# First loads of a two-branch attention kernel: 64-row slices by one broadcast DMA each, on other queues

## The chip, the cores and the metric

The kernel runs on one core of a Trainium2 chip. The time is the device time of one execution in microseconds (us), the median of several runs; a profile of one execution comes with it. Engines are called PE (matmuls; PEld is its weight load), DVE, ACT, POOL and SP. DMAs are issued by SP and ACT (hardware queues) and by POOL (software queue).

## The reference

Two attention branches over the same X (2048 rows, 576 columns, 32 heads of 18) are mixed by a gate per row. Branch A has its own keys and values for each head, branch B shares one key and one value head.

```python
g = sigmoid((x * gate_w).sum(-1, keepdims=True))
qkv = (x @ wqkv).reshape(B, S, 3, H, Dh)          # branch A
a = softmax(q @ k.T * Dh**-0.5) @ v               # per head, then @ wo
b = softmax((x @ wq) @ (x @ wk).T * Dh**-0.5) @ (x @ wv)   # then @ B_wo
return g * a + (1 - g) * b
```

All inputs are float32, and the kernel gets near float32 precision from matmuls in a rounded format (fp32r): each operand is written as a rounded high part h and a low part l = value - h, and a product takes h·h, l·h and h·l.

## The kernel before

X comes transposed (576 rows of 2048), and all projection weights but A's values come as one array `wall` of 14 row tiles, each 576 x 128. The contraction length 576 is cut into four groups of 128 (512 rows) and a fifth of 64 rows, the **slice** (rows 512 to 575). In the fifth group the 64 rows stand twice, in partitions 0 to 63 and again in 64 to 127, so that one matmul over 128 partitions does two of the three products for them: `xh[64:128, 4]` is overwritten with X's low part (L222).

`load5` (L120) fetches such a tile: the 512 rows as one DMA that SP issues (the main part), then the 64-row slice by two DMAs, one for each half of the partitions, on the queue that the argument `rest` names (SP if it is left out). `load_w` (L129) fetches a weight tile into `wst`, `load_x` (L211) a piece of X: the first two pieces are half chunks of 256 columns (`xsh`), the next three chunks of 512 (`xs`, two buffers, so the third waits until the first of them is rounded). The order is written out by hand at L224 to L237: weight tile 0 and the two half chunks with their slices on POOL's queue; six matmuls on constants that keep PE busy (L230); weight tiles 1 and 2, slices on POOL's queue as well; then the three chunks and weight tiles 3 to 5, all on SP.

`prep_w` (L134) rounds a weight tile on ACT (L126) and takes the low part on DVE (L127). `split_x` (L216) rounds 256 columns of X on ACT (L220) and takes low parts on DVE (L221, L222). The loop at L245 runs over the four chunks of 512 columns: row tiles 0, 1 and 2 are projected for each chunk (`project`, L142: matmuls of L150 into `ps`; for the first chunk row tile 0 goes in two halves of 256 columns), and within it the next chunk is rounded. A projection leaves through ACT (L154) and DVE (L160) and is written to `qk` in DRAM by a DMA of POOL (L161); for some also a `kd` write (L167). Row tiles 3 to 13 follow (`project_rest`, L268), each over all four chunks, with weight tiles fetched three row tiles ahead. After that come the attention steps, which the change doesn't touch.

The tile framework gives every DMA of the hardware queues one of eight completion semaphores in turn; the ninth waits until the first has landed, and so on. DMAs of POOL have eight of their own.

Of the kernel before, what the change touches and what calls it, by code (L numbers as in the profile page):

```python
# [11 lines left out]
AF = mybir.ActivationFunctionType  # L12
# [30 lines left out]
def gated_mix_kernel(ctx: ExitStack, tc: tile.TileContext, xT, wall, wv, wo, out):  # L43
    nc = tc.nc
    P = 128

    def dma(o, i, eng=None):
        o, i = (x.bitcast(F32) if x.dtype == F32R else x for x in (o, i))
        return (eng or nc.sync).dma_start(o, i)
# [27 lines left out]
    ones = fixed.tile([P, 32], F32, name="ones")  # L77
# [3 lines left out]
    nc.vector.memset(acc, 0.0)  # L81
    nc.vector.memset(vb, 1.0)
    nc.vector.memset(ones, 1.0)
    nc.scalar.activation(ones, ones, AF.Copy)

# [31 lines left out]

    def load5(t, src, rest=None):  # L120
        dma(t[:, 0:4, :], src[0:512, :].rearrange("(p k) m -> p k m", p=P))
        dma(t[0:64, 4, :], src[512:576, :], rest)
        dma(t[64:128, 4, :], src[512:576, :], rest)

    def split_w(st, w, eng_l):
        nc.scalar.activation(w["h"], st, AF.Copy)  # L126
# [2 lines left out]
    def load_w(mt, rest=None):  # L129
        st = wpool.tile([P, NKT, P], F32, name="wst", bufs=6)  # L130
        load5(st, wall[mt], rest)
        return st

    def prep_w(st):  # L134
        w = {y: wpool.tile([P, NKT, P], F32R, name=f"w{y}", bufs=3) for y in "hl"}
        split_w(st, w, nc.vector)
        return w
# [4 lines left out]
    def project(mt, c, w, parts=1):  # L142


        fp = ps_s.tile([P, 512], F32, name="ps")
        cs = slice(c * 512, (c + 1) * 512)
        g = 512 // parts
        for i in range(parts):
            for n, (a, b, k, kr) in enumerate(PROJ):
                nc.tensor.matmul(fp[:, g * i:g * i + g], w[a][:kr, k, :],  # L150
                                 X[b][:kr, k, c * 512 + g * i:c * 512 + g * i + g],
                                 start=(n == 0), stop=(n == len(PROJ) - 1))
        hl = stp.tile([P, 2, 512], F32R, name="phl", bufs=4)
        nc.scalar.activation(hl[:, 0, :], fp, AF.Copy)  # L154
        if mt == 0 or c == 0 and mt in HAS_K:
            st = stp.tile([P, 512], F32, name="pst", bufs=3)
            nc.scalar.activation(st, fp, AF.Copy)
            if c == 0:
                KD[mt] = st
        nc.vector.tensor_tensor(hl[:, 1, :], fp, hl[:, 0, :].bitcast(F32), op=OP.subtract)  # L160
        dma(qk_d[:, mt * P:(mt + 1) * P, cs].rearrange("a p f -> p a f"), hl, nc.gpsimd)  # L161
        if c == 1 and mt in HAS_K:
            d = stp.tile([P, 512], F32, name="pd", bufs=1)
            nc.vector.tensor_tensor(d, fp, KD.pop(mt), op=OP.subtract)
            dhl = stp.tile([P, 2, 512], F32R, name="pdhl", bufs=1)
            split(d, dhl[:, 0, :], dhl[:, 1, :], nc.scalar, nc.vector)
            dma(kd_d[:, mt * P:(mt + 1) * P, :].rearrange("a p f -> p a f"), dhl, nc.gpsimd)  # L167
        if mt == 0:
            dma(z_d[cs], st[ROW_G:ROW_G + 1, :])
            return c, st  # L170

    def shared_v(c, st):
        pv = ps_m.tile([P, 512], F32, name="pm")
        for j in range(4):
            nc.tensor.transpose(pv[:, 18 * j:18 * j + 18],  # L175
                                st[ROW_VB:ROW_VB + 18, j * P:(j + 1) * P],
                                ident[ROW_VB:ROW_VB + 18, ROW_VB:ROW_VB + 18])
        nc.vector.tensor_copy(vb[:, 4 * c:4 * c + 4, 0:18],
                              pv[:, 0:72].rearrange("p (j d) -> p j d", d=18))
# [28 lines left out]
    with tc.tile_pool(name="xs", bufs=1, side="right") as xsp:  # L208
        XS = []

        def load_x(c, rest=None):  # L211
            half = c < 2
            XS.append(xsp.tile([P, NKT, 256 if half else 512], F32, name="xsh" if half else "xs", bufs=2))
            load5(XS[c], xT[:, 256 * c:256 * c + 256] if half else xT[:, 512 * (c - 1):512 * c], rest)

        def split_x(c):  # L216
            xs = XS[c // 2 + 1][:, :, 256 * (c % 2):256 * (c % 2) + 256] if c > 1 else XS[c]
            cs = slice(c * 256, (c + 1) * 256)
            xh = X["h"][:, :, cs]
            nc.scalar.activation(xh, xs, AF.Copy)  # L220
            nc.vector.tensor_tensor(X["l"][:, :, cs], xs[:, 0:4], xh[:, 0:4].bitcast(F32), op=OP.subtract)  # L221
            nc.vector.tensor_tensor(xh[64:128, 4], xs[64:128, 4], xh[64:128, 4].bitcast(F32), op=OP.subtract)  # L222

        W = [load_w(0, nc.gpsimd)]  # L224
        load_x(0, nc.gpsimd)
        load_x(1, nc.gpsimd)

        warm = ps_m.tile([P, 512], F32, name="pm")
        for i in range(6):
            nc.tensor.matmul(warm[:, 0:304], ident, vb.rearrange("p k d -> p (k d)"), start=True, stop=True)  # L230
        W.append(load_w(1, nc.gpsimd))
        W.append(load_w(2, nc.gpsimd))
        for c in range(2, 5):
            load_x(c)
        dma(ones_r.rearrange("a (b c) -> (a b) c", c=32), ones)
        for mt in range(3, 6):
            W.append(load_w(mt))  # L237
        for t in vst:
            nc.gpsimd.memset(t, 1.0)
        WP = [prep_w(W.pop(0))]  # L240
        split_x(0)
        split_x(1)
        WP.append(prep_w(W.pop(0)))
        WP.append(prep_w(W.pop(0)))
        for c in range(4):  # L245
            keep = project(0, c, WP[0], 2 if c == 0 else 1)
            if c == 3:
                WN = prep_w(W.pop(0))
            project(1, c, WP[1])
            if c < 3:  # L250
                split_x(2 * c + 2)
                split_x(2 * c + 3)
            shared_v(*keep)
            project(2, c, WP[2])
    vwp = ph1.enter_context(tc.tile_pool(name="vwp", bufs=1, side="right"))

    def load_wv(hf):
        VS[hf] = vwp.tile([P, NKT, 288], F32, name="vwst")
        load5(VS[hf], wv[:, 288 * hf:288 * hf + 288])
# [409 lines left out]
    for T in range(0, NSTEP + 2, 2):  # L669
# [7 lines left out]
        for op in (FIRST if T == 0 else ALONE if alone else UNIT if units else PLAIN).split():  # L677
            k, second, c = op[0], op[1:2] == "B", op[2:]
# [61 lines left out]
```

## Time and profile before

| | us |
|---|---|
| median of 3 runs | 2768.68 (2768.68 to 2769.95) |
| the profiled execution | 2769.62 |
| its span, first to last instruction | 2767.8 |
| PE busy | 2755.4 |
| DVE busy | 2420.0 |
| ACT busy | 2432.1 |
| POOL busy | 214.9 |

The mean granted clock of PE was 0.998 of full speed. Times in the views count from the span's start. A row of the timeline has start, length, engine, line, operation, tiles and shapes, and in brackets the idle time before it and what ended it. A row of a window view has the stretch, its length, busy time and instructions of PE, PEld, DVE, ACT and POOL, then the granted clock, the mean busy share of the 16 DMA engines and their GB/s. A row of DMA issues has the tiles, the queue, how many, the size of one and, for POOL, the time to landing. POOL's two DMAs for one slice count as two.

### The profile page before, as it was taken

How to read it: one execution, taken by the hardware profiler on the slowest of the kernel's cores; microseconds unless marked ns; L12 is line 12 of the kernel's file. 1: busy time of each engine (PE TensorE's matmuls, PEld its weight loads, DVE VectorE, ACT ScalarE, POOL GpSimd, SP SyncE). 2: the span in 40 equal slices, each digit the busy share in tenths (PEclk: the TensorE clock that was granted, in tenths of full speed). 3: DMA queues.
4: the chain of work that ended last, by engine and by line, in shares of the span. 5: the costliest groups of instructions: out<-in, count | busy, mean ns of one | idle time of the engine just before them, and what ended most of it. 6: DMA issues, size and time to landing. Idle time of an engine off the chain costs nothing.

```text
span 2767.8 us, 57564 instructions
## 1 busy us (share of the span) xinstructions
PE 2755.4 (100%) x22158; PEld 1226.9 (44%) x22158; DVE 2420.0 (87%) x4495; ACT 2432.1 (88%) x4776; POOL 214.9 (8%) x349
## 2 busy tenths in 40 slices
PE   9999999999999999999999999999999999999999
PEld 7888333333333333333333444444444443334554
DVE  4347999999999999999999999999999999998873
ACT  3332999999999999999999999999999999998776
POOL 2220000011001000100110001000100010011000
PEclk9999999999999999999999999999999999999999
DMA  7762011121112111211143234232332223234412
GB/s 250 251 227 74 24 32 27 32 59 53 34 30 63 42 32 35 72 39 32 40 108 99 70 76 105 61 83 71 88 85 77 70 80 84 66 77 120 110 35 87
DMA packets 122962, 214.51 MB, mean 78 GB/s; under 512 B 53500, under 2 KB 80716, under 8 KB 111002
## 3 DMA queue, kind: packets, MB, share of 16 engines
q1 hardware_dynamic: 108256, 170.79, 23.6%
q0 software_dynamic: 9824, 35.07, 3.4%
q10 hardware_dynamic: 4608, 4.98, 0.5%
q8 instruction: 174, 2.85, 0.4%
q14 instruction: 100, 0.82, 0.1%
HBM read 137.23 MB, written 64.77 MB: 73 GB/s over the span
## 4 chain that ended last, share of the span: by engine, by line
PE 99%; DVE 0%; DMA 0%; ACT 0%; POOL 0%; issue 0%; DVEq 0%; POOLq 0%; ACTq 0%
PE ps L402 42%; PE acc L416 39%; PE ps L150 7%; PE pm L367 5%; PE pm L542 4%; PE ps L186 2%; DMA xsh<-xT 0%; PE ps L367 0%; PE pm L402 0%; DVE mx L376 0%; DVE oacc L554 0%; PE pm L569 0%; PE ps L592 0%; ACT pt L409 0%; PE pm L175 0%
## 5 line engine op out<-in xcount | busy, mean ns | idle before, releaser
L409 ACT ACTIVATE pt<-ps 128x512 f32<-128x512 f32 x4052 | 2129.8, 613 | 104.0 <-PE pm L367 46.4
L376 DVE TENSOR_REDUCE mx<-pm 128x1 f32<-128x512 f32 x3064 | 1957.0, 684 | 138.8 <-PE pm L367 95.2
L402 PE MATMUL ps<-qs,ksb 56*128 56x512 f32 x2688 | 906.9, 436 | 0.3
L367 PE MATMUL pm<-ksb,qs 54*128 54x512 f32 x2332 | 813.4, 443 | 0.0
L402 PEld LDWEIGHTS ps<-qs,ksb 56*128 56x128 f32 x2688 | 436.5, 184 | 688.4 <-ACT pt L409 669.3
L416 PE MATMUL acc<-pt,vb 128*19 128x256 f32 (+1 forms) x6144 | 592.4, 457 | 0.1
L416 PE MATMUL acc<-pt,vg 128*19 128x256 f32 (+1 forms) x5656 | 579.4, 481 | 0.4 <-DVE oe L428 0.4
L402 PE MATMUL ps<-qs,ksa 56*128 56x512 f32 x1364 | 456.3, 437 | 0.0
L367 PE MATMUL pm<-ksa,qs 54*128 54x512 f32 x1232 | 433.4, 443 | 0.0
L367 PEld LDWEIGHTS pm<-ksb,qs 54*128 54x128 f32 x2332 | 375.2, 184 | 2.2
L402 PEld LDWEIGHTS ps<-qs,ksa 56*128 56x128 f32 x1364 | 218.4, 184 | 344.2 <-ACT pt L409 316.8
L373 DVE CUSTOM_DVE_ANT_0 junk<-pm,xb 128x512 bf16<-128x512 f32 x500 | 340.3, 681 | 0.2 <-ACT xb L370 0.2
L370 ACT ACTIVATE xb<-pm 128x512 f32<-128x512 f32 x500 | 305.1, 610 | 0.0
L367 PEld LDWEIGHTS pm<-ksa,qs 54*128 54x128 f32 x1232 | 200.4, 184 | 0.7
L416 PEld LDWEIGHTS acc<-pt,vb 128*19 128x19 f32 x6144 | 104.2, 97 | 209.2 <-issue 199.1
L416 PEld LDWEIGHTS acc<-pt,vg 128*19 128x19 f32 x5656 | 96.5, 97 | 208.2 <-issue 195.4
L367 PE MATMUL pm<-kdb,qs 54*128 54x512 f32 x372 | 148.5, 399 | 0.0
L116 POOL CAST mh<-mt 128x32 fp32r<-128x32 f32 x64 | 13.4, 210 | 1696.0 <-DVE mt L384 1696.0
L154 ACT ACTIVATE phl<-ps 128x512 fp32r<-128x512 f32 x56 | 33.5, 597 | 104.4 <-PE ps L150 75.6
L160 DVE TENSOR_TENSOR phl<-ps,phl 128x512 fp32r<-128x512 f32 x56 | 38.7, 692 | 94.7 <-ACT phl L154 70.9
L150 PE MATMUL ps<-xh,wh 128*128 128x512 f32 (+1 forms) x285 | 83.7, 392 | 4.9 <-ACT xh L220 4.9
L150 PE MATMUL ps<-xh,wl 128*128 128x512 f32 (+1 forms) x285 | 82.9, 389 | 0.0
(107 smaller groups left out, 1373.6 us busy)
## 6 DMA issues: line engine op xcount, KB each, us to landing
qs<-qk SPq DMA_DIRECT2D x384, 144.0 KB
qk<-phl POOLq DMA_DIRECT2D x56, 512.0 KB, 4.1
ksa<-qk SPq DMA_DIRECT2D x132, 144.0 KB
ksb<-qk SPq DMA_DIRECT2D x66, 144.0 KB
onh<-oh SPq DMA_DIRECT2D x32, 256.0 KB
onl<-ol SPq DMA_DIRECT2D x32, 256.0 KB
oih<-onh SPq DMA_DIRECT2D x16, 512.0 KB
oil<-onl SPq DMA_DIRECT2D x16, 512.0 KB
```

Of the source, the lines that this page charges most:

```text
L150: nc.tensor.matmul(fp[:, g * i:g * i + g], w[a][:kr, k, :], X[b][:kr, k, c * 512 + g * i:c * 512 + g * i + g], start=(n == 0), stop=(n == ...
L154: nc.scalar.activation(hl[:, 0, :], fp, AF.Copy)
L160: nc.vector.tensor_tensor(hl[:, 1, :], fp, hl[:, 0, :].bitcast(F32), op=OP.subtract)
L186: nc.tensor.matmul(fp[:, 0:288], X[b][:kr, k, st_ * P:(st_ + 1) * P], w[a][:kr, k, :], start=(n == 0), stop=(n == len(PROJ) - 1))
L367: nc.tensor.matmul(pm, qs[u % 3][b:b + 54, i * P:(i + 1) * P], k, start=True, stop=True)
L370: nc.scalar.activation(MX["x", u, i], pm, AF.Relu)
L373: nc.vector.tensor_tensor_reduce(junk, pm, MX.pop(("x", u, i)), 1.0, -3e38, op0=OP.add, op1=OP.max, accum_out=MX[u][:, i, c:c + 1])
L376: nc.vector.tensor_reduce(MX[u][:, i, c:c + 1], pm, axis=AX.X, op=OP.max)
L402: nc.tensor.matmul(ps, kst(u)[b:b + 56, i * P:(i + 1) * P], qs[u % 3][b:b + 56, c * 512:(c + 1) * 512], start=True, stop=True)
L409: nc.scalar.activation(pt, ps, AF.Exp, scale=SCALE)
L416: nc.tensor.matmul(acc[32 * j:32 * j + 19, a:b], v_of(u, i), PT[u, i, j][:, a:b], start=(i == 0), stop=(i == 15), skip_group_check=True)
L542: nc.tensor.matmul(fp[:, 0:288], o[b][:r, t, s2 * P:(s2 + 1) * P], w[a][:r, t, 288 * hf:288 * hf + 288], start=(n == 0), stop=(n == 3 * nt ...
```

## The change

The slice comes by one DMA, whose source is a broadcast of the 64 rows to two copies. The slices of weight tile 0 and of the two half chunks of X are issued by ACT, those of weight tiles 1 and 2 by SP, like the later ones. ACT's first activation (a copy of `ones` onto itself, which brings ACT's table load with it) moves from the very start to behind ACT's three DMAs. Of the first 256 columns of X, ACT rounds groups 0 to 2 and DVE groups 3 and 4. Since ACT's and SP's DMAs share the eight semaphores of the hardware queues, in the built program the main part and the slice of weight tile 2 wait for the slice and the main part of weight tile 0; the main parts and slices of the first two full chunks wait likewise for those of the two half chunks.

```diff
-    nc.scalar.activation(ones, ones, AF.Copy)
...
     def load5(t, src, rest=None):
         dma(t[:, 0:4, :], src[0:512, :].rearrange("(p k) m -> p k m", p=P))
-        dma(t[0:64, 4, :], src[512:576, :], rest)
-        dma(t[64:128, 4, :], src[512:576, :], rest)
+        dma(t[:, 4, :], src[512:576, :].unsqueeze(0).to_broadcast([2, 64, src.shape[1]]), rest)
...
-            nc.scalar.activation(xh, xs, AF.Copy)
+            if c == 0:
+                nc.scalar.activation(xh[:, 0:3], xs[:, 0:3], AF.Copy)
+                nc.vector.tensor_copy(xh[:, 3:5], xs[:, 3:5])
+            else:
+                nc.scalar.activation(xh, xs, AF.Copy)
...
-        W = [load_w(0, nc.gpsimd)]
-        load_x(0, nc.gpsimd)
-        load_x(1, nc.gpsimd)
+        W = [load_w(0, nc.scalar)]
+        load_x(0, nc.scalar)
+        load_x(1, nc.scalar)
+        nc.scalar.activation(ones, ones, AF.Copy)
...
-        W.append(load_w(1, nc.gpsimd))
-        W.append(load_w(2, nc.gpsimd))
+        W.append(load_w(1))
+        W.append(load_w(2))
```

## The prediction

> **What bounds the kernel now.** I read the page first, for the engine that carries the chain.
>
> ```profile
> span 2767.8 us, 57564 instructions
> PE   9999999999999999999999999999999999999999
> PE 99%; DVE 0%; DMA 0%; ACT 0%; POOL 0%; issue 0%; DVEq 0%; POOLq 0%; ACTq 0%
> ```
>
> TensorE (PE) is busy in every slice and 99% of the chain is its own work. Whatever delays PE once delays the end by as much; whatever lies beside it costs nothing. The change touches only the opening, so I read the chain of waits there (start, length, what), and the matmuls that open each chunk of 512 columns in the timeline.
>
> ```profile
> 2.74 0.50 POOL xsh L49
> 3.25 8.08 DMA xsh<-xT
> ...
> 11.40 1.28 ACT xh L220
> ...
> 12.72 8.86 PE ps L150 x42
> ```
>
> ```profile
> 1.92 5.90 PE L230 MATMUL pm<-vb,ident 128*128 128x304 f32 x12 [1.92 <-DVE ones L83]
> 6.83 0.74 ACT L126 ACTIVATE wh<-wst 128x640 fp32r<-128x640 f32 x1 [4.57 <-DMA wst<-wall]
> 22.11 2.43 ACT L220 ACTIVATE xh<-xs 128x1280 fp32r<-128x1280 f32 x2
> 25.18 1.07 PE L150 MATMUL ps<-xh,wh 128*128 128x512 f32 x4
> 35.30 1.07 PE L150 MATMUL ps<-xh,wh 128*128 128x512 f32 x4
> 45.41 1.07 PE L150 MATMUL ps<-xh,wh 128*128 128x512 f32 x4
> ```
>
> The only load that PE waits for is the first half chunk of X: its 64-row slice, issued by POOL, lands at 11.3 us, ACT rounds it, and PE, idle since 7.82 (1.92 + 5.90), starts at 12.72. From there PE goes on without a stop: chunk 1 starts at 25.18, chunk 2 at 35.30, chunk 3 at 45.41, 10.12 apart. Chunk 1 is rounded by ACT from 22.11 to 24.54, 0.6 us before PE takes it; chunks 2 and 3 go the same way.
>
> **The change, part by part.** *How many DMA engines a slice uses.* Before, a slice is two DMAs of 64 rows. After, it is one whose source is a broadcast: in the built program it reads as 2 copies, 64 rows, columns, with the 2 outermost and of stride zero. Before has no such load of 2 copies, but it has a broadcast of one row to 18 (R, L49), with 18 outermost. These stretches hold only that and other 18-row loads (DMA share, GB/s at the end of a row):
>
> ```profile
> 598.00:600.00 2.00, 2.00 (x16) 0.62 (x14) 1.83 (x5) 1.78 (x5) 0.00 (x0) 1.00 0.58 139
> 600.00:602.00 2.00, 2.00 (x24) 0.77 (x24) 2.00 (x4) 2.00 (x5) 0.00 (x0) 1.00 0.61 156
> ...
> 604.00:606.00 2.00, 2.00 (x22) 0.76 (x24) 2.00 (x4) 1.95 (x5) 0.00 (x0) 1.00 0.61 143
> ...
> R<-r_d SPq DMA_DIRECT2D x7, 144.0 KB
> ```
>
> With these loads queued the share stays at 0.58 to 0.61, where the stretches below, with 16 engines at work, show 1.02 to 1.09. That is 9 of 16 engines (0.56 times 1.02 to 1.09 is 0.57 to 0.61), and 9 is the largest divisor of 18 below 16. So the outermost count limits the engines, and a zero stride doesn't lift that. I take **2 engines** for every slice of the changed kernel. The other end, 16, is possible, because no row shows a load whose source says 2 and whose destination says 128; it is rival A.
>
> *What one engine moves.* Loads of the opening, the weights among others, with all 16 at work:
>
> ```profile
> 2.00:3.00 1.00, 1.00 (x2) 0.73 (x3) 0.00 (x0) 0.25 (x2) 1.00 (x3) 1.00 0.78 263
> ...
> 6.00:7.00 1.00, 1.00 (x3) 0.68 (x2) 0.00 (x0) 0.17 (x1) 0.52 (x1) 1.00 1.06 350
> 7.00:8.00 1.00, 0.82 (x3) 0.22 (x1) 0.41 (x1) 0.56 (x1) 0.97 (x3) 1.00 1.09 360
> 8.00:13.00 5.00, 0.28 (x1) 0.28 (x2) 0.72 (x2) 1.60 (x2) 0.49 (x2) 0.76 1.05 292
> 33.00:34.00 1.00, 1.00 (x6) 0.82 (x5) 0.53 (x2) 1.00 (x2) 0.98 (x2) 1.00 1.02 394
> 34.00:35.00 1.00, 1.00 (x6) 0.83 (x5) 0.97 (x2) 0.70 (x1) 0.13 (x1) 1.00 1.06 393
> ```
>
> Divided by 16: 22.2 GB/s from 6 to 8 (21.7 KB a us), 18.2 from 8 to 13 (17.8 KB), 24.6 from 33 to 35 (24.0 KB). The R stretches give 146/9 = 16.3 GB/s (15.9 KB). I take 21.7 KB for loads, the row with the same 1 KB rows of X, and keep 24.0 and 17.8 as ends. Transfers run from about 2.0 us, as the row from 2 to 3 shows.
>
> *The load on the two engines.* A main part spreads over 16 engines, a slice over 2. Sizes of before:
>
> ```profile
> wst<-wall SPq DMA_DIRECT2D x3, 256.0 KB
> xsh<-xT SPq DMA_DIRECT2D x2, 512.0 KB
> xs<-xT SPq DMA_DIRECT2D x2, 1024.0 KB
> xs<-xT SPq DMA_DIRECT2D x4, 128.0 KB
> xsh<-xT POOLq DMA_DIRECT2D x4, 64.0 KB, 7.9
> wst<-wall POOLq DMA_DIRECT2D x6, 32.0 KB, 6.5
> qk<-phl POOLq DMA_DIRECT2D x56, 512.0 KB, 4.1
> ```
>
> Each is half a slice, so on one of the two engines a weight tile is 256/16 + 32 = 48 KB, a half chunk of X 32 + 64 = 96, a full chunk 64 + 128 = 192, a qk write 32. Up to the end of chunk 1 the engine carries three weight tiles, two half chunks and a chunk: 144 + 192 + 192 = **528 KB**, 24.3 us. With 1.3 us (32/24.0) for a qk write of chunk 0 in between, chunk 1 has landed at 2.0 + 24.3 + 1.3 = 27.6. ACT's 2.43 follow: PE starts chunk 1 at 30.0 in place of 25.18, **4.8 us late**. The order in which the ACT and SP queues share the engine doesn't matter for this sum, since all of it is ahead. Nor do the waits that the built order puts on SP (third weight tile for the first one's slice, chunk 1 for the first half chunk's): the engine has other queued work then.
>
> *The next rounds.* For each further chunk the two engines move 192 KB (8.8 us) and three qk writes (3 x 1.3 = 4.0), 12.8 us, while PE needs 10.12: **2.7 late** again. In the first of these rounds a kd write of equal size adds 1.3, so it costs **4.0**. Chunk 2 starts 8.8 late, chunk 3 11.5. After that a weight tile of 48 KB (2.2 us) is due per row tile of four projections, some 13 us, each with a qk write (5.3 us together), and it is asked for three row tiles ahead: no further wait.
>
> *Costed at nothing.* The first PE matmuls: 3 of them no longer wait for the slice, and after it lands comes a DVE copy of 128x512 in place of ACT's 1.28. That price is not in the trace; between DVE's 0.42 (64x256, below) and 0.69 (128x512) I take 0.5. But by the split of the engine between two queues the first slice lands at 12 or 13 us, so PE goes on about where it did, the second half chunk starts some 3 us later than before, and chunk 0 ends near 29. All of this is hidden by chunk 1, which isn't there before 30.0; with that cover gone it would cost those 3 to 4 us.
>
> ```profile
> 13.95 0.42 DVE L222 TENSOR_TENSOR xh<-xsh,xh 64x256 fp32r<-64x256 f32 x1
> 19.53 0.69 DVE L160 TENSOR_TENSOR phl<-ps,phl 128x512 fp32r<-128x512 f32 x1 [1.85 <-ACT pst L157]
> 0.73 1.28 ACT L84 ACT_TABLE_LOAD   x1 [0.73 <-PEq L732]
> 197.70 0.35 ACTq L49 DMA_DIRECT2D v_d<-vst  x1
> 0.73 0.40 SPq L49 DMA_DIRECT2D wst<-wall  x1
> 20.52 0.75 POOL L49 DMA_DIRECT2D qk<-phl  x1 [12.03 <-DVE phl L160]
> ```
>
> ACT's three issues (0.35 to 0.7 each) and the moved table load (1.28) fill it from 0.73 to 4.3 at most; its first tile comes after 6.8. POOL loses ten issues and has nothing else to do before 20.52. SP issues one slice DMA in place of two, about 0.4 less each time, and no chain passes through SP's issuing.
>
> The **sum** is 4.8 + 4.0 + 2.7 = 11.5 us. The profiled execution took 2769.62, 0.94 above the median 2768.68; on the median the forecast is **2780**. With 24.0 KB a us the terms are 2.5, 3.2 and 1.9 (7.6, or 2776); with 17.8 they are 10.2, 6.0 and 4.7 (20.9, or 2790).
>
> **The rivals.**
>
> *A, faster: the slices spread over 16 engines* because the destination's 128 rows decide. Then everything for the first half chunk, 960 KB with its weights, has come at 2.0 + 983/355 = 4.8 us plus landing, rounding is done near 7, and PE starts when the warm-up ends, 7.82: up to 4.90 gained. The idle gap that lowered its clock goes too.
>
> ```profile
> 9.00:10.00 1.00, 0.00 (x0) 0.00 (x0) 0.00 (x0) 0.00 (x0) 0.00 (x0) 1.00 1.02 262
> 11.00:12.00 1.00, 0.00 (x0) 0.00 (x0) 0.00 (x0) 0.60 (x1) 0.00 (x0) 0.50 1.08 330
> 16.00:17.40 1.40, 1.40 (x9) 1.40 (x8) 1.37 (x3) 0.00 (x0) 0.00 (x0) 0.50 1.03 317
> 17.40:18.40 1.00, 1.00 (x9) 1.00 (x9) 0.28 (x1) 0.00 (x0) 0.00 (x0) 1.00 1.07 354
> ```
>
> The granted clock (before the share) is 0.50 until 17.4, and chunk 0 takes 25.18 - 12.72 = 12.46, against 10.12 for chunk 1: 2.3 more. Gain 4.9 to 7.2, time 2762 to 2764; I name 2763. The forecast turns into this from four engines on: a chunk then costs 64 + 256/4 = 128 KB (5.9 us) plus 4.0, which fits in 10.12. For it speaks that no row has this shape; against it, the R rows. The Trainium skill, DMA: Bandwidth & Descriptors, section Rules for kernel authors, says that two transfers to partition halves should be one of 128 partitions, which is what this change does, and by which 2763 would be the result. The same page's section on why a DMA increments its semaphore by 16 says that the number of engines divides the outermost count of both sides, which by that rule is 2; the R rows agree with it at 9 for 18.
>
> *B, slower still:* two engines at the rate of the R rows, 15.9 KB. Terms 13.7, 7.3 and 6.0, together 27 us: 2796. Against it: those are rows of 8 KB, not 1 or 2.
>
> *C, mostly hidden:* two engines, but the qk writes go in beside the loads and take nothing from them. A round is then 8.8 us, less than PE's 10.12, and only 4.8 - 1.3 = 3.5 at chunk 1 is left: 2772. For it: shares above 1; against it: none is over 1.09.
>
> **How the numbers follow.** Forecast 0.68, B 0.07, C 0.12, A 0.13. About 0.2% (5.5 us) can be told from no change. The forecast and B are slower by more, with 0.02 of C; the rest of C and half of A lie within; the other part of A is faster: 0.77, 0.15, 0.08. The range 2770 to 2791 holds the forecast with both its rate ends, and C; it leaves out A and B, 0.20.
>
> **What would show it.** Right: PE opens chunks 1, 2 and 3 at about 30, 44 and 57, each after ACT's L222 waiting for xs; the DMA share falls to 0.1 to 0.2 between the main parts (two engines of 16), and SP's chunk 1 load is issued after the first slice has landed. Wrong: a PE start near 8 with the clock at 1.00 (A); chunk 1 late but chunks 2 and 3 not later (C); waits for wst or phl after 60 us, which I cost at nothing.

## The result, and the profile after

The changed kernel takes 2780.64 us (median of 6 runs, 2779.22 to 2782.05), before takes 2768.92 (6 runs): a ratio of 1.0042, 95% interval 1.0032 to 1.0053. That is slower by more than 0.2%, and 0.6 us from the forecast of 2780. The profiled execution took 2782.05 with a span of 2780.2, 12.4 more than the span before.

The head of the page of the changed kernel and PE's row of slices:

```profile
span 2780.2 us, 57523 instructions
...
PE   7999999999999999999999999999999999999999
```

Nearly all of the loss lies in the first slice: 11.9 us of it are there at 60.50 us (read below), 12.4 at the end. The chain of waits of that stretch (start, length, what):

```profile
1.91 9.77 DMA xsh<-xT
...
11.69 0.57 SPq L49
...
12.31 14.36 DMA xs<-xT
...
32.13 20.32 DMA xs<-xT
```

Before, this chain held one load, the first half chunk, and then PE alone. Now it holds that load, landing at 11.68, then SP's issue of chunk 1, which waited for it through the shared semaphores, and the first and the third full chunk of X, landing at 26.67 and 52.45. The prediction had named this issue and put no price on its wait. The timeline of the changed kernel, with the matmuls that open chunks 1, 2 and 3 and the roundings ahead of them:

```profile
12.18 0.58 PE L148 MATMUL ps<-xh,wh 128*128 128x256 f32 x1 [4.17 <-DVE xh L220]
18.56 1.22 PE L148 MATMUL ps<-xh,wh 128*128 128x256 f32 x4 [3.40 <-ACT xh L222]
26.76 2.45 ACT L222 ACTIVATE xh<-xs 128x1280 fp32r<-128x1280 f32 x2 [0.82 <-DMA xs<-xT]
29.26 1.20 PE L148 MATMUL ps<-xh,wh 128*128 128x512 f32 x4 [0.20 <-ACT xh L222]
37.58 2.44 ACT L222 ACTIVATE xh<-xs 128x1280 fp32r<-128x1280 f32 x2 [0.98 <-DMA xs<-xT]
40.08 1.21 PE L148 MATMUL ps<-xh,wh 128*128 128x512 f32 x4 [0.39 <-ACT xh L222]
52.54 2.43 ACT L222 ACTIVATE xh<-xs 128x1280 fp32r<-128x1280 f32 x2 [5.07 <-DMA xs<-xT]
55.02 2.07 PE L148 MATMUL ps<-xh,wh 128*128 128x512 f32 x4 [4.47 <-ACT xh L222]
60.50 1.09 PE L148 MATMUL ps<-xh,wh 128*128 128x512 f32 x4
```

ACT waits for `xs` ahead of all three chunks, and PE waits for ACT. Against 25.18, 35.30 and 45.41 before, the chunks open 4.1, 4.8 and 9.6 us late. The last row is the next projection of chunk 3; before it stood here:

```profile
48.58 1.07 PE L150 MATMUL ps<-xh,wh 128*128 128x512 f32 x4
```

So it is 11.9 late: chunk 3's first projection took 5.5 us in place of 3.2. The windows of the changed kernel show why (granted clock, DMA share and GB/s are the last three columns):

```profile
10.00:11.50 1.50, 0.00 (x0) 0.00 (x0) 0.00 (x0) 0.00 (x0) 0.00 (x0) 1.00 0.14 47
...
31.00:32.40 1.40, 1.40 (x8) 1.14 (x7) 1.31 (x4) 0.00 (x0) 0.00 (x0) 1.00 0.13 54
52.00:52.40 0.40, 0.00 (x0) 0.00 (x0) 0.00 (x0) 0.00 (x0) 0.00 (x0) 1.00 0.15 51
52.00:54.00 2.00, 0.00 (x0) 0.00 (x0) 0.15 (x1) 1.46 (x2) 0.00 (x0) 0.72 0.14 51
...
56.00:58.00 2.00, 2.00 (x6) 1.57 (x5) 1.91 (x4) 0.00 (x0) 0.00 (x0) 0.50 0.32 108
```

The clock fell to 0.50 while PE stood idle and stayed there for its next matmuls. And where PE waits for a chunk, or between the main parts, the DMA share is 0.13 to 0.15, with 47 to 54 GB/s: two engines of 16 are 0.125. The share is 0.14 already from 10.00 to 11.50, ahead of SP's issue at 11.69, so the two engines had work queued while SP waited.

### The profile page after: what moved, and what is told of

It reads as the page before. It is cut to its first block, busy times and chain, and to the rows that moved or that the text cites. A ratio compares the mean times of both kernels' runs of the same rounds, so it can differ in the third digit from the quotient of the medians.

```text
span 2780.2 us, 57523 instructions
## 1 busy us (share of the span) xinstructions
PE 2759.9 (99%) x22158; PEld 1227.2 (44%) x22158; DVE 2420.3 (87%) x4496; ACT 2436.1 (88%) x4776; POOL 210.1 (8%) x339
## 4 chain that ended last, share of the span: by engine, by line
PE 96%; DMA 2%; DVE 1%; ACT 0%; SPq 0%; issue 0%; ACTq 0%; POOL 0%; DVEq 0%
PE ps L405 41%; PE acc L419 38%; PE ps L148 5%; PE pm L545 4%; PE pm L370 4%; PE ps L184 2%; DMA xs<-xT 1%; DMA xsh<-xT 0%; DMA ot<-oe 0%; DMA R<-r_d 0%; PE ps L370 0%; PE pm L405 0%; DMA qs<-qk 0%; DVE mx L379 0%; SPq L49 0%; DVE oacc L557 0%
```

## The experiments

The theory: a slice goes over as many DMA engines as its source has outermost entries, two here, and the queue on those two makes the chunks of X late. Rival Q: the moved queues and the shared semaphores make the chunks late. Rival R: a source with a zero stride, read twice, is slow in itself. All times are medians, with the kernel before run beside them: 2769.50 for the first four kernels, 2769.09 for the next four, 2768.53 for the last two.

| kernel | us | ratio to before, 95% interval |
|---|---|---|
| source read 64 rows outermost | 2763.83 | 0.9981 (0.9972 to 0.9990) |
| two DMAs per slice, new queues | 2766.34 | 0.9988 (0.9979 to 0.9997) |
| before with the broadcast alone | 2776.43 | 1.0024 (1.0015 to 1.0034) |
| fillers that read `vb` | 2785.59 | 1.0058 (1.0045 to 1.0070) |
| chunk slices as two DMAs | 2773.62 | 1.0017 (1.0008 to 1.0026) |
| four outermost | 2768.56 | 0.9998 (0.9989 to 1.0007) |
| fillers that read `ident` | 2779.66 | 1.0037 (1.0025 to 1.0050) |
| rows twice in the inputs | 2763.54 | 0.9979 (0.9970 to 0.9988) |
| rows twice, POOL's queue | 2766.72 | 0.9992 (0.9983 to 1.0000) |
| rows twice, ACT rounds alone | 2763.60 | 0.9983 (0.9974 to 0.9992) |

**The outermost count: 2, 4, 64.** One line of the changed kernel differs.

```diff
-  dma(t[:, 4, :], src[512:576, :].unsqueeze(0).to_broadcast([2, 64, src.shape[1]]), rest)
+  dma(t[:, 4, :], src[512:576, :].unsqueeze(1).to_broadcast([64, 2, src.shape[1]]), rest)
```

> The changed kernel with one thing altered: the slice's broadcast source is read as 64 rows, 2 copies, columns instead of 2 copies, 64 rows, columns. Still one DMA per slice, the same queues, waits and bytes; each row then stands in two neighbouring partitions, so the products of the 64-row group are not the reference's. Theory (engines of a DMA follow the outermost count of its source, so 2 before and 16 here): no chunk waits for X, PE starts near 8 us, time 2762 to 2764. Rival Q (the moved queues and the shared semaphores delay the chunk loads): about 2780, as the changed kernel. Rival R (a zero-stride source is slow in itself): about 2780.

```diff
+  dma(t[:, 4, :], src[512:544, :].unsqueeze(0).to_broadcast([4, 32, src.shape[1]]), rest)
```

> The changed kernel with each slice read as 4 copies of 32 rows, so with 4 outermost in place of 2; the same bytes and DMAs, but the lower 32 rows of the 64-row group take the place of the upper ones, and its products are not the reference's. Theory: 4 engines, a chunk costs the busiest of them 128 KB and three qk writes, 10 us, about what PE needs: between the kernel with 16 engines and the one before, 2764 to 2769. Rival (any broadcast over copies is slow, or the count plays no part): about 2780.

2763.83 with 64 outermost, 2768.56 with 4, 2780.64 with 2. The windows, first of the kernel with 4 outermost, then of the one with 64:

```profile
9.50:11.00 1.50, 0.53 (x4) 0.53 (x5) 0.91 (x2) 0.00 (x0) 0.00 (x0) 1.00 0.27 94
```

```profile
8.00:10.00 2.00, 0.55 (x4) 0.55 (x5) 1.00 (x2) 0.96 (x2) 0.00 (x0) 1.00 1.06 373
10.00:12.00 2.00, 1.96 (x16) 1.75 (x15) 1.89 (x3) 2.00 (x3) 0.00 (x0) 1.00 1.00 360
```

While PE waits for the first half chunk the share is 0.14 with two outermost and 0.27 with four, and the rate is 47 and 94 GB/s. With 64 the loads keep all 16 engines busy. Bytes, queues, waits and the number of DMAs are the same in all three, and all three read rows more than once. That settles the theory and rules out Q and R as the cause of the loss. The openings of the chunks in the kernel with 4 (chunks 1, 2, 3):

```profile
25.53 1.07 PE L148 MATMUL ps<-xh,wh 128*128 128x512 f32 x4
...
35.64 1.07 PE L148 MATMUL ps<-xh,wh 128*128 128x512 f32 x4
...
45.76 1.07 PE L148 MATMUL ps<-xh,wh 128*128 128x512 f32 x4
```

None waits, and they are 10.11 apart: from four engines on the rounds fit, the point that the prediction worked out. What is left, 0.35 us late, comes from the start.

**Two DMAs per slice, new queues kept.**

```diff
-  dma(t[:, 4, :], src[512:576, :].unsqueeze(0).to_broadcast([2, 64, src.shape[1]]), rest)
+  dma(t[0:64, 4, :], src[512:576, :], rest)
+  dma(t[64:128, 4, :], src[512:576, :], rest)
```

> The changed kernel with the slice loaded by two DMAs of 64 rows, as before the change; queues and rounding as changed. Theory: 16 engines for each, 2762 to 2766, a little behind one DMA over 16 engines because more DMAs share the eight semaphores. Rival Q (moved queues): about 2780.

2766.34, 0.3 over the range of the theory and far from Q. The queues and the rounding as changed, without the broadcast, gain 3 us.

**The chunk slices alone as two DMAs.** In the changed kernel `load_x` asks for two DMAs of 64 rows when it loads a full chunk.

> The changed kernel, but the slices of the three full chunks come as two DMAs of 64 rows (16 engines); the first weight tiles' and half chunks' slices stay broadcasts of 2 copies. Theory: the slip of the start, which I costed at nothing because chunk 1 hid it, now shows by itself: PE opens chunk 1 near 29 us (4 late), waits for no chunk after that, and its clock isn't lowered again; 2772 to 2773. Rival (the chunk slices have no part in it): 2780.

2773.62, 0.6 over the range. Its chunks 1 and 2 open so:

```profile
29.02 1.07 PE L152 MATMUL ps<-xh,wh 128*128 128x512 f32 x4
...
39.13 1.07 PE L152 MATMUL ps<-xh,wh 128*128 128x512 f32 x4
```

Chunk 1 is 3.8 late, and so is chunk 2. This is the slip of the start that the changed kernel hides behind chunk 1. So with the chunk slices on 16 engines 4.5 us of the loss remain (2773.62 - 2769.09), from the slices that stay broadcasts; the other 7 (2780.64 - 2773.62) hang on the chunk slices.

**The broadcast alone, in the kernel before.** `load5` as changed, all else as before.

> The kernel before with one thing altered: the slice by one broadcast DMA of 2 copies; first slices still on POOL's queue. Theory: the chunk slices use 2 engines, but SP issues chunks 1 and 2 early, so 304 KB per busy engine up to chunk 1 land near 17 us, and chunk 2 and 3 each have a full round in advance: 2767 to 2772. Rival R (zero-stride source slow in itself) or the broadcast as the whole cause: about 2780.

2776.43: a miss. The chunk part held, the end did not. The timeline of this kernel, PE and then ACT and SP, and last a step of its chain:

```profile
14.79 1.23 PE L149 MATMUL ps<-xh,wh 128*128 128x256 f32 x4 [7.42 <-ACT xh L219]
...
27.44 1.07 PE L149 MATMUL ps<-xh,wh 128*128 128x512 f32 x4
...
47.96 1.20 PE L149 MATMUL ps<-xh,wh 128*128 128x512 f32 x4
...
57.45 0.61 PE L174 MATMUL pm<-ident,pst 18*128 18x18 f32 x4 [2.80 <-ACT pst L156]
57.99 2.08 PE L149 MATMUL ps<-xh,wh 128*128 128x512 f32 x4
...
62.65 1.08 PE L149 MATMUL ps<-xh,wh 128*128 128x512 f32 x4
```

```profile
45.47 2.44 ACT L219 ACTIVATE xh<-xs 128x1280 fp32r<-128x1280 f32 x2 [0.72 <-DMA xs<-xT]
...
56.80 0.60 ACT L156 ACTIVATE pst<-ps 128x512 f32<-128x512 f32 x1 [4.70 <-DMA z_d<-pst]
```

```profile
31.87 16.71 SPq L49 DMA_DIRECT2D wst<-wall  x6
48.63 9.01 SPq L49 DMA_DIRECT2D z_d<-pst  x4
```

```profile
48.63 8.15 DMA z_d<-pst
```

PE starts 2.1 late, since the one POOL slice lands after the two of before did. Chunks 1 and 3 open 2.3 and 2.5 late, so the loads of the chunks cost next to nothing, as expected. Then ACT wants one of the three `pst` buffers back, which the small store `z_d` still holds. That store stands on SP behind six weight DMAs that took 16.7 us to issue, three of them slices over two engines, and once issued it took another 8.15 us to land. The projection behind that wait takes 4.7 us (57.99 to 62.65) in place of 3.3 before, with the clock lowered once more (0.62 from 57 to 59, 0.53 from 59 to 61). I had counted the engines' load and not SP's queue behind it. The theory stands, but that the slow slices reach PE here as well, through SP's queue and this store, is read from the timeline; no run took it apart.

**The lowered clock.** Fillers are put ahead of chunk 3's first projection, so that PE isn't idle there.

```diff
+            if c == 3:
+                fill = ps_m.tile([P, 512], F32, name="pm")
+                for _ in range(4):
+                    nc.tensor.matmul(fill[:, 0:304], ident, vb.rearrange("p k d -> p (k d)"), ...)
```

> The changed kernel with four constant matmuls (about 4 us of PE) put ahead of chunk 3's first projection, inside the 4.5 us in which PE waits for that chunk. Theory: the wait itself (9.6 us late at chunk 3) stays, but the clock isn't lowered behind it, and the 2.3 us that chunk 3's first projection took longer go away: 2778. Rival (the clock has no part, the 12 us are all load time): 2780 to 2781.

```diff
+                for _ in range(9):
+                    nc.tensor.matmul(fill[:, 0:128], ident, ident, ...)
```

> The changed kernel with nine constant matmuls of 128 columns (near 4 us of PE) ahead of chunk 3's first projection. They read only the identity tile, so nothing holds them behind the load, as the fillers of the first trial were held. Theory: chunk 3 opens at 55 us as before, at full clock, and the 2.3 us of the lowered clock go: 2778 to 2779. Rival (the clock has no part): 2780 to 2781.

The first missed its aim: 2785.59. Its fillers read `vb`, which DVE writes only after it has split chunk 3, so they came behind the load. The timelines, first of that kernel, then of the second:

```profile
57.72 4.05 PE L252 MATMUL pm<-vb,ident 128*128 128x304 f32 x8 [7.37 <-DVE vb L176]
```

```profile
50.51 2.17 PE L252 MATMUL pm<-ident 128*128 128x128 f32 x18
55.28 1.21 PE L148 MATMUL ps<-xh,wh 128*128 128x512 f32 x4 [2.60 <-ACT xh L222]
...
58.62 1.07 PE L148 MATMUL ps<-xh,wh 128*128 128x512 f32 x4
```

The second did what it should: chunk 3 opens at 55.28 and its first projection takes 3.3 us in place of 5.5, so the next begins at 58.62 and not at 60.50, 1.9 earlier. The median is 2779.66, only 1.0 below the changed kernel's 2780.64, above the 2778 to 2779 expected and nearer to the rival's 2780. In the profiled pair the clock's part is shown. It is no oddity of one execution: the mean granted clock is 0.996 in five of the changed kernel's six executions and 0.997 in all five with these fillers. How many microseconds it is worth in a typical execution stays open, since the changed kernel's profiled execution is its slowest of six.

**A better version, and which part of it counts.** The inputs hold the 64 rows twice, so that a slice is one plain DMA of 128 rows.

```diff
+  dma(t[:, 4, :], src[512:640, :], rest)
...
+    for k in ("xT", "wv"):
+        arrays[k] = np.concatenate([arrays[k], arrays[k][512:]], axis=0)
+    arrays["wall"] = np.concatenate([arrays["wall"], arrays["wall"][:, 512:]], axis=1)
```

> The changed kernel with the 64 rows laid out twice in the input arrays, so that a slice is one plain DMA of 128 rows; it computes all that the reference does. Theory: the same as the source read with 64 rows outermost, 16 engines: 2763 to 2764, ahead of both kernels. Rival (repeated reading of the same rows is what costs, or saves): differs from that by more than 1.5 us.

> The kernel before, with one plain DMA of 128 rows per slice (rows laid out twice in the inputs); first slices still on POOL's queue, ACT rounds alone. It separates the queue from the number of DMAs. Theory: the first half chunk's slice is POOL's second DMA in place of its fourth and lands some 2 us earlier than the 11.3 of before, so 2766 to 2768. Rival (moving the queue to ACT is what brings the 5.5 us of the last kernel): 2769, as before.

> The kernel with rows laid out twice and ACT's queue, but without the shared rounding of the first half chunk: ACT alone rounds it. Theory: PE starts 0.4 us later (1.26 against 0.84 on ACT): 2764. Rival (the shared rounding carries the gain): 2767 or more.

2763.54 on ACT's queue, 2766.72 on POOL's with ACT rounding alone, and 2763.60 on ACT's queue without the shared rounding. The first beats both kernels. The shared rounding brings nothing that can be measured. The timelines of the first two, with the window from 10 to 18 of each (ACT's queue, then POOL's), and the first projection of the third:

```profile
9.40 0.74 PE L148 MATMUL ps<-xh,wh 128*128 128x256 f32 x4 [1.62 <-ACT xh L219]
```

```profile
10.00:18.00 8.00, 7.94 (x48) 6.53 (x47) 5.48 (x8) 4.83 (x7) 0.93 (x1) 1.00 0.88 324
```

```profile
9.84 1.22 PE L149 MATMUL ps<-xh,wh 128*128 128x256 f32 x4 [2.70 <-ACT xh L219]
```

```profile
10.00:18.00 8.00, 8.00 (x37) 7.68 (x38) 5.35 (x7) 3.62 (x5) 0.00 (x0) 0.62 0.90 332
```

```profile
8.21 0.74 PE L148 MATMUL ps<-xh,wh 128*128 128x256 f32 x4
```

PE starts only 0.4 us earlier with ACT's queue. The larger part of the 3 us between them goes with the clock: it stays at 1.00 over a gap of 1.62 us in the one profile and has fallen, to a mean of 0.62, after one of 2.70 in the other. This is read from the two profiles; no run took it apart. The start itself varies by more than that: without the shared rounding PE was expected to start 0.4 us later and starts at 8.21, 1.2 earlier, though the medians agree. The first kernel's profiled execution is its slowest of eleven (2764.46), so differences of a microsecond between single profiles of the start are not to be read.

## Why the prediction was right

- **Two engines per slice: right**, and shown by the shares of 0.14, 0.27 and 1.00 for 2, 4 and 64 outermost. The Trainium skill's rule on the number of engines (DMA: Bandwidth & Descriptors, section on why a DMA increments its semaphore by 16) gives the same counts. The Trainium skill's rule for two transfers to partition halves (the same page, section Rules for kernel authors), one transfer of 128 partitions in their place, held only where the source had 128 or 64 rows outermost (2763.5 and 2763.8, against 2766.3 with two).
- **Chunk 1, 4.8 late: 4.1.** It landed at 26.67, forecast 27.6.
- **Chunk 2, 4.0 more: 0.7. Chunk 3, 2.7 more: 4.8.** Together 5.5 against 6.7. I put three qk writes and the kd write into the first round and three into the second. The issues of the changed kernel on POOL in these rounds (one more follows at 48.49), and from its DMA views of 26.7 to 37.5 us and of 37.5 to 52.45 us, the two rounds, what POOL's queue moved (packets, MB, share of 16 engines):

```profile
24.07 0.93 POOL L49 DMA_DIRECT2D qk<-phl  x1 [21.89 <-DVE phl L158]
26.97 0.74 POOL L49 DMA_DIRECT2D qk<-phl  x1 [1.96 <-DVE phl L158]
32.74 0.73 POOL L49 DMA_DIRECT2D qk<-phl  x1 [5.03 <-DVE phl L158]
...
45.80 0.73 POOL L49 DMA_DIRECT2D qk<-phl  x1 [1.51 <-DVE phl L158]
```

```profile
q0 software_dynamic: 220, 0.77, 18.3%
...
q0 software_dynamic: 962, 3.49, 58.4%
```

  A write is 512 KB, 0.52 MB. So the first round, up to the landing of chunk 2 at 37.5, had one and a half writes (issued at 24.07 and 26.97), and the second, up to 52.45, had six and a half (32.74 to 45.80, the kd write among them, four left out above, and part of the one at 48.49). The first round took 10.9 us in place of 14.1, the second 14.9 in place of 12.8. Their sum, 25.8, is near the 26.9 that I had; its division was off. That the writes make the difference between the rounds fits these counts; no run changed the writes alone.
- **The rate of one engine: a little low.** I took 22.2 GB/s from stretches with 16 engines at work; the windows from 10.00 and from 52.00 to 52.40, with loads alone, show 47 and 51 for the two together, 23.5 and 25.5 each.
- **Costed at nothing.** The start: PE went on at 12.18, the second half chunk opened at 18.56, 2.7 later than before (the row below, of the kernel before), both hidden behind chunk 1; with the cover taken away it cost 3.8, forecast 3 to 4. Issuing: the prediction said that no chain passes through SP's; this one does, at 11.69, but the two engines were at work through that wait. Waits behind 60 us: the loss grows there only from 11.9 to 12.4.

```profile
15.87 1.05 PE L150 MATMUL ps<-xh,wh 128*128 128x256 f32 x4
```

- **Missed: the clock.** The stall ahead of chunk 3 lowered it, and 2.3 us came on top in the profile. I had priced the clock's part for rival A and not for the stalls of my own forecast. With it the loss in the profile is 9.6 + 2.3 = 11.9, against my 11.5: the chunk terms were 1.9 too large and the clock 2.3 too small, and the two nearly cancel. The 0.6 us between forecast and result say less than the range does.
- **Rival A's price** of 2763 is what the kernels with 16 engines reached (2763.54, 2763.83), though PE starts at 9.40 and 9.45 there and not at 7.82: the clock, which stays up, makes up the rest. (Its chance of 0.13 went 0.05 to no change and 0.08 to faster, and not in halves.) Rival C fell, since even the round with one and a half writes took 10.9 us, more than its 8.8, and the one with six and a half 14.9. Rival B fell with the rate.

## What to carry to other kernels

Count the engines of a DMA before merging two into one: where the merged form put a broadcast of two copies outermost, on SP's and ACT's queues, the same bytes went over two engines, and everything behind them on those two waited. Where data is needed twice, put a long count outermost if the rows may change their places in the partitions (here they may not), or lay the rows out twice in the input. Price a stall at its length plus the slower clock behind it, if the trace shows that the clock falls, and follow the queue behind a slow load to the small stores that hold buffers.

## What the runs showed of the hardware beyond that

ACT's first DMA issue took 1.14 us with 2 outermost (and with 4), 0.64 with 64 and 0.41 for the plain DMA of 128 rows; the timelines of the changed kernel and of the one with 64 outermost:

```profile
0.74 1.14 ACTq L49 DMA_DIRECT2D wst<-wall  x1
```

```profile
0.73 0.64 ACTq L49 DMA_DIRECT2D wst<-wall  x1
```

It stands ahead of the issue of the first half chunk's slice in the changed kernel; what it costs there was not taken apart. PE's clock fell near 52.9 us (a mean of 0.72 from 52 to 54 is 0.9 us at 1.00 and 1.1 at 0.50), about 4.5 - 2.1 = 2.4 us into the 4.47 us of waiting that end at 55.02, while a gap of 1.62 us left it up in one profile. The length of the gap alone does not decide: in the kernel with POOL's queue the clock fell some 2.1 us into a gap of 2.70 (the gap begins at 9.84 - 2.70 = 7.14, and a mean of 0.70 from 9.00 to 9.50 is 0.2 us at 1.00), yet it stayed at 1.00 over gaps of 2.60 with the fillers that read `ident` and with 64 outermost:

```profile
9.45 0.74 PE L148 MATMUL ps<-xh,wh 128*128 128x256 f32 x4 [2.60 <-ACT xh L219]
```

On POOL's queue the broadcast of two copies also landed later than the two DMAs it replaced (PE at 14.79 against 12.72); how many engines that queue gave it wasn't tried. With several slices under way from 10 to 13 us, that queue's packets took 27.6% of 16 engines' time, more than the 12.5% of two, so the count seen on SP's and ACT's queues is not shown for POOL's.
